# Forming the low parts of the first layer's weights on GpSimd, with a new written order for the start of the kernel

## Chip, cores and metric

One core of a Trainium2 chip runs the whole program. The metric is device time in microseconds. The kernel before was timed three times: 861.56, 856.57 and 857.43 us, median 857.43. A fourth execution, the profiled one, took 856.71 us; its span from the first to the last instruction is 854.8 us.

Engine names as the profile has them: PE is TensorE (matmul), PEld its weight loads, DVE is VectorE, ACT is ScalarE, POOL is GpSimd, SP is SyncE, which here issues the DMAs.

## What is computed

```
kv  = einsum('bhsd,bhse->bhde', k, v)            # b=4, h=8, s=576, d=64
o   = einsum('bhsd,bhde->bhse', q, kv)
x   = o / sqrt(mean(o*o, -1) + 1e-6) * g_norm    # -> 2304 tokens x 512
h   = x @ w_in1                                  # 512 x 2048
g   = h * tanh(softplus(h))                      # mish
x2  = g @ w_out1                                 # 2048 x 512
h2  = x2 @ w_in2;  g2 = max(h2,0) + alpha*min(h2,0)
out = g2 @ w_out2
```

The inputs come as 64-bit floats; the kernel reads them as pairs of 32-bit words.

## The kernel before

Every product of the two MLPs is made of three PE passes over fp32r operands, a rounded high part and the low part that is left: high x high, high x low, low x high (function `three`, lines 128 to 132). So each operand, weight or activation, needs a high part, which ACT forms by a rounding copy, and a low part, which is source minus high, one subtraction of a 128x512 tile.

A weight tile of 128x512 goes through these steps: a DMA brings its 64-bit words into a stage tile `ws`; ACT scales the high words (`w_scale`, L390, "A" in the written order); DVE puts the fp32 number together by three integer instructions (`w_bits`, L396, L397, L400, "D") in a tile `wf`, of which there are two in turn; ACT rounds it (`w_high`, L435, "H"); DVE subtracts (`w_low`, L439, "L"). Activations: mish is ACT's L505, which writes one of two tiles `n`; `g_split` rounds on ACT (L498) and subtracts on DVE (L499, the tile `gl`).

The tokens go in five blocks (512, 256, 512, 512, 512). In a block the first MLP runs over 16 slots, one for each 128 of the 2048 hidden units: slot s makes the first product of slot s (`mm1`, 12 matmuls), mish of slot s-1, the split of s-2 and the second product of s-4 (`mm2`, 12 matmuls). All weights of the first MLP are prepared in the first block, two tiles in each slot, (1, s+2) of the first layer in `mid` and (2, s-2) of the second in `last`, and kept in SBUF. `w_begin` and `w_end` (lines 443 to 454) hold a tile's high and low part back until the next tile has its bits. In slots 8 to 15 the attention of block 1 is made beside this (`hook`), with its own rows on DVE: L322 to L333 in slots 10 and 11, L345 and L363 in slots 13 and 14.

Ahead of slot 4 lies a start stage whose order is a written list, `START` (lines 44 to 49). Each entry is a letter for a step and its indices: K, k, T, t, O, s, M, l, n, f make the attention of block 0 for one pair of heads; x and y split the normed tokens (`x_split` rounds on ACT, L358; `x_low` subtracts on DVE, L363); A, D, H, L prepare a weight tile, where c0 to c3 are the first layer's weights for hidden units 0 to 511 (one tile for each 128 rows of w_in1, home `w1first`), w4 and w5 the next tiles of the first layer, u0 and u1 tiles of the second; Pcj is the three matmuls of token chunk c and slot j; g is mish and G its split. P3j needs x3 and the low parts of chunk 3.

Up to slot 20 (`MANUAL`) each engine's order is the written one. After that only PE's is, and a scheduler sets the others. GpSimd does little in the kernel before: some memory setting at the start, and subtractions in preparing the second MLP's weights from 227 us on.

Of the kernel before, what the change touches and what calls it, by code (L numbers as in the profile page):

```python
# [13 lines left out]
ALU = mybir.AluOpType  # L14
# [28 lines left out]
FIRST = "p0 c0 p1 c1 p2 p3 c2 c3 w4 u0 w5 u1".split()  # L43
START = """
W9 K0 k0 W1 T0 t0 W2 Ac0 O0 Dc0 s0 W2 K1 M0 k1 Hc0 Lc0 T1 l0 t1 n0 O1 V f0 K2 s1 x0 M1 k2 Ac1 y0 T2 l1
Dc1 t2 n1 O2 f1 K3 s2 Hc1 M2 k3 x1 Lc1 Ac2 T3 y1 l2 P01 Dc2 P02 t3 P12 n2 Hc2 O3 Ac3 f2 s3 M3 Lc2 x2
y2 P00 P03 Dc3 P10 P11 P13 l3 P20 P21 Z n3 Hc3 f3 P22 P23 Lc3 x3 Aw4 y3 Au0 Dw4 P30 P31 P32 P33 g0
G0 Hw4 Lw4 Du0 g1 G1 Hu0 Aw5 Lu0 g2 Dw5 Au1 Hw5 Du1 Lw5
""".split()


# [1 line left out]
def attn_moe_moe2(  # L53
# [30 lines left out]
    nc = tc.nc  # L84
# [41 lines left out]
    f32 = lambda t: t.bitcast(F32)  # L126

    def three(ps, lhs, rhs, start, stop, **kw):
        (lh, ll), (rh, rl) = lhs, rhs
        nc.tensor.matmul(ps, lh, rh, start=start, stop=False, **kw)  # L130
        nc.tensor.matmul(ps, lh, rl, start=False, stop=False, **kw)  # L131
        nc.tensor.matmul(ps, ll, rh, start=False, stop=stop, **kw)  # L132
# [3 lines left out]
    xh, xl = {}, {}  # L136
    at = {}
# [17 lines left out]
    def load_kv(b, p):  # L155
        R = S // KVJ
        for nm, src in (("k", k), ("v", v)):
            cols = 2 * KVJ * D
            t = room(nm, F32, cols) if b == 0 else kvp.tile([P, cols], F32, tag=nm, name=nm)
            t = t.rearrange("p (h j d) -> p h j d", h=2, j=KVJ)  # L160
            nc.sync.dma_start(
                out=t[:R], in_=src[b, 2 * p : 2 * p + 2, :, :].rearrange("h (p j) d -> p h j d", j=KVJ)
            )
            kvt[nm, b, p] = t[:R]
# [36 lines left out]
    def bank(tag, nm):  # L201
        if tag == "at":
            turn[0] += 1
            tag = f"at{turn[0] % 2}"
        pool = ps_h if tag == "h" else ps_a if tag[:2] == "at" else ps_acc
        return pool.tile([P, 512], F32, tag=tag, name=nm)
# [143 lines left out]
    def x_split(i, p, src):  # L350
        T = BLOCKS[i]
        if (i, 0) not in xh:
            x = xp.tile([P, 8 * TM], F32R, tag="x", name="x")
            for c in range(NP):
                xh[i, c] = x[:, 2 * c * TM : 2 * c * TM + T]
                xl[i, c] = x[:, (2 * c + 1) * TM : (2 * c + 1) * TM + T]
        h = xh[i, p]
        nc.scalar.copy(out=h, in_=src)  # L358
        if i:
            x_low(i, p, src)  # L360

    def x_low(i, p, src):
        nc.vector.tensor_tensor(out=xl[i, p], in0=src, in1=f32(xh[i, p]), op=ALU.subtract)  # L363

    def stage(nm, dt, cols):
        return st.tile([P, 2 * DM], dt, tag="ws", name=nm, bufs=3)[:, :cols]
# [58 lines left out]
    def w_parts(L, which, j):  # L425
        s = wst[L, which, j]
        if which:
            return *w_home(L, which, j), s
        w_home(L, 1, 0)
        w = w1[L, "first"]  # L430
        return w[:, :, 0, j, :], w[:, :, 1, j, :], s.rearrange("p (j f) -> p j f", j=EARLY)

    def w_high(L, which, j):
        h, _, s = w_parts(L, which, j)
        nc.scalar.copy(out=h, in_=s)  # L435

    def w_low(L, which, j):
        h, l, s = w_parts(L, which, j)
        nc.vector.tensor_tensor(out=l, in0=s, in1=f32(h), op=ALU.subtract)  # L439

    begun = []

    def w_end():
        while begun:
            w = begun.pop()
            w_high(*w)
            w_low(*w)

    def w_begin(*w):

# [12 lines left out]
    def at_slot(kk):  # L463
        i = kk // NJ
        return i, kk % NJ, BLOCKS[i]

    def mm1(kk, chunks=range(4)):
        i, j, T = at_slot(kk)
        if chunks[0] == 0:
            hps[kk] = bank({2: "at1", 3: "acc3"}.get(kk, "h"), "h")  # L470
        ps = hps[kk]
        wh, wl = w1[0, j]
        for c in chunks:
            cs = slice(c * P, (c + 1) * P)
            three(ps[:, :T], (wh[:, cs], wl[:, cs]), (xh[i, c], xl[i, c]), c == 0, c == NP - 1)
# [409 lines left out]
    for i in range(1, NB):  # L885
        h0, step, dk, do, dm, db = WHEN[i]
        h0 += (i - 1) * 2 * NJ
        for p in range(NP):
            h = h0 + p * step
# [71 lines left out]
    def slot(s):  # L961
        run(early, s)
        mm1(s)
        run(hook, 2 * s)
        run(after, s)
        run(late, s)
        front(s)
        run(mid, s)
        run(fin, s)
        back(s)  # L970
        run(hook, 2 * s + 1)
        run(last, s)
# [36 lines left out]
    def warm(n):  # L1009
# [18 lines left out]
        "f": f_ev,  # L1028
        "x": lambda p: x_split(0, p, at["x", p]),
        "y": lambda p: x_low(0, p, at["x", p]),  # L1030
        "A": w_scale,
        "D": w_bits,
        "H": w_high,
        "L": w_low,
        "P": lambda c, j: mm1(j, (c,)),
        "Z": lambda: nc.scalar.preload_act_table_set("mish"),
        "g": mish,
# [2 lines left out]
    with tc.manual_schedule():  # L1040
        nc.scalar.preload_act_table_set("abs_reciprocal_sqrt_and_small")
        for n in FIRST:
            if n[0] == "p":
                load_kv(0, int(n[1]))
                load_q(0, int(n[1]))
            else:
                load_w(0, code[n[0]], int(n[1:]), True)
            if n == "p1":
                for h in range(2):
                    nc.sync.dma_start(out=gcol[h * D : (h + 1) * D, :], in_=g_norm.rearrange("(p o) -> p o", o=1))  # L1050
        nc.sync.dma_start(out=acol, in_=alpha.rearrange("(j p) -> p j", p=P))
        make_identity(nc, ident)
        nc.vector.memset(ones_bd, 0.0)
        nc.vector.memset(ones_m, 0.0)
        for h in range(2):
            r = slice(h * D, (h + 1) * D)
            nc.vector.memset(ones_bd[r, r], 1.0 / D)
            nc.vector.memset(ones_m[r, 16 * h : 16 * h + 16], 1.0 / D)
        nc.vector.memset(epsb, EPS * 2.0**-SHIFT)
        nc.gpsimd.memset(keep[:, : 5 * P], 0.0)  # L1060
        nc.vector.memset(neglo, 0.0)
        for p in range(NP):
            for h in range(2):
                r = 32 * p + 16 * h
                rows = pick[p][:, h * D : (h + 1) * D]
                nc.vector.tensor_copy(out=rows, in_=ident[:, r : r + 1].to_broadcast([P, D]))
                nc.vector.tensor_tensor(
                    out=rows, in0=f32(rows), in1=ident[:, r + 1 : r + 2].to_broadcast([P, D]), op=ALU.add
                )
                nc.vector.tensor_tensor(out=neglo, in0=neglo, in1=ident[:, r + 1 : r + 2], op=ALU.subtract)  # L1070
        for n in START:
            if n[0] in "ADHL":
                w = (0, code[n[1]], int(n[2:]))
                first[n[0]](*w)
            else:
                first[n[0]](*(int(c) for c in n[1:]))
        begun.append((0, 2, 1))
        for s in range(EARLY, MANUAL):
            slot(s)
# [35 lines left out]
```

## Time and profile before

| | value |
|---|---|
| median of 3 runs | 857.43 us (856.57 to 861.56) |
| profiled execution | 856.71 us, span 854.8 us |
| PE busy | 832.7 us (97%) |
| DVE busy | 537.1 us (63%) |
| ACT busy | 314.1 us (37%) |
| POOL busy | 41.8 us (5%) |

The busy shares are means over the whole program. A change in the first block is read from the stretches of that block, and there from what PE waits for and who that one waits for. In the rows below, a timeline row shows the start in us, the duration in us, engine, line, operation, output <- inputs with shapes, and in brackets how long the engine had been idle and which engine's instruction released it. A row with x2 is two instructions merged. [...]

### The profile page before, as it was taken

The numbers are of one execution on the slowest core, as the hardware profiler recorded it, in microseconds if no ns is written. First come the engines' busy times: TensorE is split into PE (matmuls) and PEld (weight loads), VectorE is DVE, ScalarE is ACT, GpSimd is POOL, SyncE is SP. The second block draws the span as 40 slices with busy tenths as digits, with TensorE's granted clock in tenths as the row PEclk, the third lists the DMA queues.
The fourth block names the chain that finished last, engine by engine and source line by source line (L and its number), as shares of the span: only waits on it lengthen the run. The fifth ranks groups of instructions, "written<-read, shape, count | busy, mean of one in ns | idle before, by whom it ended". The sixth has DMA issues, their size and how long they took to land.

```text
span 854.8 us, 11671 instructions
## 1 busy us (share of the span) xinstructions
PE 832.7 (97%) x4408; PEld 711.5 (83%) x4408; DVE 537.1 (63%) x1017; ACT 314.1 (37%) x619; POOL 41.8 (5%) x52
## 2 busy tenths in 40 slices
PE   7999889989999999999999999999999999999997
PEld 5677668888878887888888888888988988998896
DVE  6988966372246242635697887889665568655644
ACT  4766445434333443234465323234211124111111
POOL 0000000000210303020300000000000000000000
PEclk9999999999999999999999999999999999999999
DMA  9766454414331233026996623241321231411212
GB/s 250 222 172 205 139 150 102 110 27 106 100 112 25 77 109 135 1 94 231 404 357 231 209 63 134 97 137 39 125 61 38 62 123 39 140 44 38 74 38 74
DMA packets 84744, 104.59 MB, mean 122 GB/s; under 512 B 34768, under 2 KB 58832, under 8 KB 84688
## 3 DMA queue, kind: packets, MB, share of 16 engines
q1 hardware_dynamic: 84688, 103.84, 39.2%
q8 instruction: 35, 0.57, 0.3%
q14 instruction: 21, 0.17, 0.1%
HBM read 79.70 MB, written 24.12 MB: 121 GB/s over the span
## 4 chain that ended last, share of the span: by engine, by line
PE 82%; DVE 8%; DMA 4%; SPq 2%; ACT 2%; issue 1%; DVEq 0%; ACTq 0%
PE acc L130 13%; PE acc L132 13%; PE acc L131 13%; PE h L130 7%; PE h L131 6%; PE h L132 6%; PE pp L130 6%; PE pp L132 6%; PE pp L131 6%; DMA v<-in_v_dram 2%; SPq L183 2%; PE kvps L214 1%; DVE wf L397 1%; DVE wf L400 1%; DMA k<-in_k_dram 1%
## 5 line engine op out<-in xcount | busy, mean ns | idle before, releaser
L130 PE MATMUL acc<-gh,w 128*128 128x512 f32 (+1 forms) x320 | 119.6, 374 | 0.8 <-ACT n L505 0.4
L132 PE MATMUL acc<-gh,w 128*128 128x512 f32 (+1 forms) x320 | 118.0, 369 | 0.0
L131 PE MATMUL acc<-gl,w 128*128 128x512 f32 (+1 forms) x320 | 117.9, 369 | 0.0
L499 DVE TENSOR_TENSOR gl<-n,gh 128x512 fp32r<-128x512 f32 (+1 forms) x80 | 52.2, 652 | 89.9 <-ACT gh L498 89.6
L130 PE MATMUL h<-x,w 128*128 128x512 f32 (+1 forms) x240 | 91.5, 381 | 5.6 <-ACT n L505 5.6
L132 PE MATMUL h<-x,w 128*128 128x512 f32 (+1 forms) x240 | 89.7, 374 | 0.6 <-DVE w L439 0.5
L131 PE MATMUL h<-x,w 128*128 128x512 f32 (+1 forms) x240 | 89.6, 373 | 0.0
L132 PE MATMUL acc<-w,g 128*128 128x512 f32 x216 | 85.4, 395 | 0.0
L498 ACT CAST gh<-n 128x512 fp32r<-128x512 f32 (+1 forms) x80 | 46.1, 577 | 100.4 <-PE acc L132 99.9
L766 ACT CAST g<-ty 128x384 fp32r<-128x384 f32 x48 | 24.7, 515 | 138.4 <-DVE ty L764 136.5
L130 PEld LDWEIGHTS acc<-gh,w 128*128 128x128 f32 x320 | 60.3, 188 | 11.9 <-ACT n L505 0.9
L132 PEld LDWEIGHTS acc<-gh,w 128*128 128x128 f32 x320 | 60.3, 188 | 10.6 <-DVE w L439 0.4
L131 PEld LDWEIGHTS acc<-gl,w 128*128 128x128 f32 x320 | 60.4, 189 | 9.6
L505 ACT ACTIVATE n<-h 128x512 f32<-128x512 f32 (+1 forms) x80 | 44.5, 556 | 45.3 <-DVE gl L499 44.6
L130 PEld LDWEIGHTS h<-x,w 128*128 128x128 f32 x240 | 45.9, 191 | 17.3 <-ACT n L505 6.9
L131 PE MATMUL acc<-w,g 128*128 128x512 f32 x144 | 56.6, 393 | 0.0
L131 PE MATMUL acc<-w,xb 128*128 128x512 f32 x144 | 56.6, 393 | 0.0
L130 PE MATMUL acc<-w,g 128*128 128x512 f32 x144 | 56.0, 389 | 0.0
L130 PE MATMUL acc<-w,xb 128*128 128x512 f32 x144 | 56.0, 389 | 0.0
L132 PEld LDWEIGHTS h<-x,w 128*128 128x128 f32 x240 | 45.9, 191 | 9.5 <-DVE w L439 1.6
L131 PEld LDWEIGHTS h<-x,w 128*128 128x128 f32 x240 | 45.8, 191 | 7.4
L132 PEld LDWEIGHTS acc<-w,g 128*128 128x128 f32 x216 | 40.5, 188 | 9.4 <-DVE g L767 0.9
(216 smaller groups left out, 1700.2 us busy)
## 6 DMA issues: line engine op xcount, KB each, us to landing
xb<-wd SPq DMA_DIRECT2D x72, 256.0 KB, 2.7
ws<-in_moe_w_out_dram SPq DMA_DIRECT2D x32, 512.0 KB, 4.3
ws<-in_moe_w_in_dram SPq DMA_DIRECT2D x16, 512.0 KB, 4.8
r<-in_moe_w_in_dram SPq DMA_DIRECT2D x12, 512.0 KB, 3.9
wd<-r SPq DMA_DIRECT2D x12, 512.0 KB, 2.6
w<-wd SPq DMA_DIRECT2D x12, 512.0 KB, 6.0
k<-in_k_dram SPq DMA_DIRECT2D x16, 288.0 KB, 3.8
v<-in_v_dram SPq DMA_DIRECT2D x16, 288.0 KB, 4.2
```

The source lines that it names most:

```text
L130: nc.tensor.matmul(ps, lh, rh, start=start, stop=False, **kw)
L131: nc.tensor.matmul(ps, lh, rl, start=False, stop=False, **kw)
L132: nc.tensor.matmul(ps, ll, rh, start=False, stop=stop, **kw)
L183: nc.sync.dma_start(out=t[r : r + 32, C * p0 : C * (p0 + n)].rearrange("p (b d) -> p b d", d=32), in_=q[b, h, s : s + C * n, d : d + 32].r ...
L214: nc.tensor.matmul(ps[hs, hs], kt[:, h, j, :], vt[:, h, j, :], start=(j == 0), stop=(j == KVJ - 1))
L397: nc.vector.scalar_tensor_tensor(out=si, in0=high, scalar=-0x80000000, in1=si, op0=ALU.bitwise_and, op1=ALU.bitwise_or)
L400: nc.vector.scalar_tensor_tensor(out=si, in0=high, scalar=3, in1=si, op0=ALU.logical_shift_left, op1=ALU.bitwise_or)
L498: nc.scalar.copy(out=gh, in_=g)
L499: nc.vector.tensor_tensor(out=gl, in0=g, in1=f32(gh), op=ALU.subtract)
L505: nc.scalar.activation(out=g, in_=hps.pop(kk)[:, :T], func=AF.Mish)
L766: nc.scalar.copy(out=h, in_=out)
```

## The change

Thirty-three subtractions go from DVE to GpSimd: the low parts of c1, c2, c3, w4, u0 and w5 in the start stage (new letter Q), two of the four token chunks' low parts (x1 and x2, new letter z), and every low part that `w_end` forms (u1 and the 24 tiles of slots 4 to 17). c0, x0 and x3 stay on DVE. `START` is written anew: P00 stands ahead of O2, the bits of w4 (Dw4) stand ahead of the norm of the last pair (n3, f3), and w4 and u0 get their high and low parts earlier as seen from the first mish.

```diff
 START = """
 W9 K0 k0 W1 T0 t0 W2 Ac0 O0 Dc0 s0 W2 K1 M0 k1 Hc0 Lc0 T1 l0 t1 n0 O1 V f0 K2 s1 x0 M1 k2 Ac1 y0 T2 l1
-Dc1 t2 n1 O2 f1 K3 s2 Hc1 M2 k3 x1 Lc1 Ac2 T3 y1 l2 P01 Dc2 P02 t3 P12 n2 Hc2 O3 Ac3 f2 s3 M3 Lc2 x2
-y2 P00 P03 Dc3 P10 P11 P13 l3 P20 P21 Z n3 Hc3 f3 P22 P23 Lc3 x3 Aw4 y3 Au0 Dw4 P30 P31 P32 P33 g0
-G0 Hw4 Lw4 Du0 g1 G1 Hu0 Aw5 Lu0 g2 Dw5 Au1 Hw5 Du1 Lw5
+t2 Dc1 P00 n1 O2 f1 K3 s2 Hc1 Qc1 M2 k3 x1 z1 Ac2 T3 P01 l2 t3 Dc2 P02 O3 Hc2 Qc2 n2 Ac3 f2 s3 P03 M3
+x2 z2 Aw4 Dc3 l3 P10 P11 P12 P13 Hc3 Qc3 Dw4 n3 f3 Z Au0 P20 P21 P22 P23 x3 y3 Hw4 Qw4 P30 P31 P32 P33
+Du0 Aw5 g0 G0 Hu0 Qu0 g1 Dw5 g2 G1 Au1 Hw5 Qw5 Du1
 """.split()
...
-    def x_low(i, p, src):
-        nc.vector.tensor_tensor(out=xl[i, p], in0=src, in1=f32(xh[i, p]), op=ALU.subtract)
+    def x_low(i, p, src, e=nc.vector):
+        e.tensor_tensor(out=xl[i, p], in0=src, in1=f32(xh[i, p]), op=ALU.subtract)
...
-    def w_low(L, which, j):
+    def w_low(L, which, j, e=nc.vector):
         h, l, s = w_parts(L, which, j)
-        nc.vector.tensor_tensor(out=l, in0=s, in1=f32(h), op=ALU.subtract)
+        e.tensor_tensor(out=l, in0=s, in1=f32(h), op=ALU.subtract)
...
             w_high(*w)
-            w_low(*w)
+            w_low(*w, nc.gpsimd)
...
+        "z": lambda p: x_low(0, p, at["x", p], nc.gpsimd),
...
+        "Q": lambda *w: w_low(*w, nc.gpsimd),
```

In DVE's order of the start stage, from the norm of head pair 2 (L305, L306) on, the difference is this (q is the normed tile, wf a weight being put together):

```order
 L305 SCALAR_TENSOR_TENSOR q<-u,q 128x512
 L306 SCALAR_TENSOR_TENSOR q<-ops,gneg,q 128x512
-L439 TENSOR_TENSOR w1first<-wf,w1first 128x4x128
-L363 TENSOR_TENSOR x<-q,x 128x512
+L396 TENSOR_SCALAR wf<-ws 128x512
+L397 SCALAR_TENSOR_TENSOR wf<-ws,wf 128x512
+L400 SCALAR_TENSOR_TENSOR wf<-ws,wf 128x512
```

The low parts of c2 and x2 are gone from this place. Two preparations, c3 and w4, now stand in a row ahead of the norm of pair 3, where one did.

In a slot of the first block DVE's rows stood like this before (two finished subtractions `w`, one weight's bits, the activation's low part `gl`, the next weight's bits):

```order
L439 TENSOR_TENSOR w_569<-wf,w_569 128x512
L439 TENSOR_TENSOR w_606<-wf,w_606 128x512
L396 TENSOR_SCALAR wf<-ws 128x512
L397 SCALAR_TENSOR_TENSOR wf<-ws,wf 128x512
L400 SCALAR_TENSOR_TENSOR wf<-ws,wf 128x512
L499 TENSOR_TENSOR gl<-n,gh 128x512
```

Both L439 rows are gone from DVE; L396, L397, L400, L499 and again L396 to L400 stand there without a break.

GpSimd's order, from its last memory setting on, begins with these rows (w_430 is w4, w_456 u0, w_472 w5):

```order
L1062 MEMSET keep 128x640
L439 TENSOR_TENSOR w1first<-wf,w1first 128x4x128
L363 TENSOR_TENSOR x<-q,x 128x512
L439 TENSOR_TENSOR w_430<-wf,w_430 128x512
L439 TENSOR_TENSOR w_456<-wf,w_456 128x512
L439 TENSOR_TENSOR w_472<-wf,w_472 128x512
```

The first two kinds of rows alternate as c1, x1, c2, x2, c3 in the program; 28 `w` rows follow and then the rows that were there before.

## Rows read from the trace of the kernel before

**Rows 1.** Stretches: start:end; busy us (rows) of PE, PEld, DVE, ACT, POOL; clock, DMA
```profile
28.40:37.70 9.30, 9.30 (x41) 7.33 (x39) 8.35 (x14) 7.17 (x12) 0.00 (x0) 1.00 0.56 149
37.70:46.70 9.00, 7.56 (x51) 5.15 (x50) 8.43 (x16) 6.44 (x12) 0.00 (x0) 1.00 0.32 117
46.70:84.00 37.30, 37.30 (x239) 29.96 (x236) 31.49 (x53) 24.31 (x53) 0.00 (x0) 1.00 0.73 207
84.00:97.00 13.00, 13.00 (x58) 10.72 (x58) 12.26 (x26) 4.86 (x9) 0.00 (x0) 1.00 0.43 135
97.00:119.70 22.70, 17.23 (x63) 12.71 (x62) 18.41 (x35) 11.61 (x23) 0.00 (x0) 0.86 0.49 148
```

**Rows 2.** Timeline of PE, the first matmul after its longest stop
```profile
116.69 0.64 PE L130 MATMUL h<-x,w 128*128 128x512 f32 x1 [2.76 <-ACT n L505]
```

**Rows 3.** Waits, PE from 20, others from 0 us: total us, times, longest
```profile
PE h L130 <- ACT n L505: 5.2, 4, 2.8
DVE w L439 <- ACT w L435: 5.8, 9, 0.9
SPq L378 <- DVE wf L400: 26.3, 10, 4.6
```

**Rows 4.** Instructions of tile w, first 140 us: durations in ns, min/median/max
```profile
L439 DVE TENSOR_TENSOR w<-wf,w x28: 681/688/694, 37.8 to 138.9; 128x512 fp32r<-128x512 f32 x28
```

**Rows 5.** Timeline of ACT and DVE in the start stage
```profile
22.95 0.70 ACT L390 ACTIVATE ws<-ws 128x512 f32<-128x512 f32 x1
...
32.78 0.75 DVE L306 SCALAR_TENSOR_TENSOR q<-ops,gneg,q 128x512 f32<-128x512 f32 x1
33.45 0.68 DVE L439 TENSOR_TENSOR w1first<-wf,w1first 128x512 fp32r<-128x512 f32 x1
33.57 0.62 ACT L358 CAST x<-q 128x512 fp32r<-128x512 f32 x1 [1.21 <-DVE q L306]
34.22 0.70 DVE L363 TENSOR_TENSOR x<-q,x 128x512 fp32r<-128x512 f32 x1
```

**Rows 6.** Timeline of DVE in slots 13 and 14
```profile
109.02 0.42 DVE L396 TENSOR_SCALAR wf<-ws 128x512 int32<-128x512 int32 x1
...
110.27 0.69 DVE L400 SCALAR_TENSOR_TENSOR wf<-ws,wf 128x512 int32<-128x512 int32 x1
110.88 0.68 DVE L499 TENSOR_TENSOR gl<-n,gh 128x512 fp32r<-128x512 f32 x1
111.48 0.47 DVE L345 SCALAR_TENSOR_TENSOR qT<-o,gcol,bps 128x256 f32<-128x256 f32 x1
...
117.18 0.69 DVE L439 TENSOR_TENSOR w<-wf,w 128x512 fp32r<-128x512 f32 x1 [0.58 <-ACT w L435]
```

**Rows 7.** Groups of POOL by form: busy us, mean ns of one | idle before
```profile
L576 POOL TENSOR_TENSOR r<-wf,r 128x512 fp32r<-128x512 f32 x10 | 13.2, 1319 | 55.8 <-ACT r L575 55.8
```

**Rows 8.** Timelines of POOL and DVE where both work, in later blocks
```profile
321.11 0.74 POOL L621 TENSOR_TENSOR r<-wf 128x256 f32<-128x256 f32 x1
321.22 1.17 DVE L249 TENSOR_TENSOR qs<-qT,qs 128x512 fp32r<-128x512 f32 x1 [0.83 <-ACT qs L248]
321.93 1.06 POOL L622 TENSOR_TENSOR wf<-r,wf 128x256 f32<-128x256 f32 x1
...
387.62 1.29 POOL L576 TENSOR_TENSOR r<-wf,r 128x512 fp32r<-128x512 f32 x1 [3.53 <-ACT r L575]
388.14 1.32 DVE L397 SCALAR_TENSOR_TENSOR xw<-xw 128x512 int32<-128x512 int32 x1 [1.40 <-ACT xw L390]
...
423.74 0.97 DVE L396 TENSOR_SCALAR xw<-xw 128x512 int32<-128x512 int32 x1
```

**Rows 9.** Timeline of PE: last chunk's first product, slot 4's first, slot 5's first
```profile
35.03 0.39 PE L130 MATMUL h<-x,w1first 128*128 128x512 f32 x1
...
37.75 0.48 PE L130 MATMUL h<-x,w 128*128 128x512 f32 x1
...
46.73 0.50 PE L130 MATMUL h<-x,w 128*128 128x512 f32 x1
```

## What I predict, before the run

> **What bounds the kernel now.** I read the table of stretches first, to find where TensorE (PE) stands still near the code that changes. From 46.7 to 84 us it is busy all the time, and VectorE (DVE) is busy 31.49 of 37.3 us. From 97 to 119.7 us PE is busy only 17.23 of 22.7 us, at a mean granted clock of 0.86, and from 37.7 to 46.7 us 7.56 of 9.0 us [rows 1]. So the first block has two places where time can be won, about 5.5 us and 1.4 us of standing still, and the lost clock. In the second place the matmuls that follow a stop last 0.64 us [rows 2] and stand at half speed, the 1.2 GHz level; a clock of 0.86 over 22.7 us means that about 28% of it was at half speed, so some 3.2 us of work were lost. Everything else in the program (the other 700 us) is not touched except by the order in which the scheduler then puts rows.
>
> The list of waits says who makes PE wait: the mish on ScalarE (ACT), 5.2 us in 4 pieces, the longest 2.8 us [rows 3]. The mish in turn waits for DVE, which frees its two `n` buffers with `gl` (L499). DVE works in written order, and `gl` stands in line behind the weight preparation. DVE itself waits for ACT to round a weight (L435) before it can form the low part (L439): 5.8 us in 9 pieces [rows 3]. So in these stretches DVE is what matters, and the reader should see its queue as the path.
>
> **The price that leaves DVE.** 33 subtractions go: 28 of `w` at 0.688 us [rows 4], three of `w1first` and two of `x` at the same price (0.68 and 0.70 us, [rows 5]). From start to start on a full DVE one takes 0.61 to 0.77 us [rows 5, 6]; I take 0.61 (0.67 in the start stage). By stretch: 8 before 46.7 us, 12 up to 84 us, 9 up to 119.7 us, 4 after.
>
> **The price that comes.** The same shape and types on GpSimd (POOL) take 1.32 us in ten cases [rows 7], 1.29 us undisturbed. POOL had nothing else to do there, so its own time costs nothing; each low part has at least one slot (over 6 us) until it is read. What costs is that the two engines exclude each other, and the trace shows it. A DVE subtraction that starts 0.11 us behind a POOL one takes 1.17 us instead of 0.69 and ends 0.54 us after POOL's end; POOL's next one, issued meanwhile, ends 0.60 us after DVE's end and takes 1.06 us for 0.74 us. L397 beside a 512-wide POOL row takes 1.32 us and ends 0.55 us after POOL's end. The shift L396 takes 0.97 us instead of 0.42 beside POOL [rows 6, 8]. So they alternate: POOL holds about 1.29 - (0.74 - 0.60) = 1.15 us, then DVE's op needs 0.55 us. On a full DVE the next row would have ended 0.79 us after the one before (0.10 gap and 0.69); with POOL between it ends 1.15 + 0.55 = 1.70 us after. **One POOL subtraction delays a full DVE by 0.9 us** and takes 0.61 us off it. The bounds are 0 (it falls into an idle time of DVE) and 0.9.
>
> Which DVE rows are held up is partly unknown: all rows seen beside POOL have two inputs in SBUF or are the fast shift. Rows with one input in PSUM (L301, L306, L345) never stand beside POOL in this trace; bounds 0 and 0.9 us. They differ from every blocked row in just that input, so I take 0 and keep 0.9 for the range. The Trainium skill (SBUF — State Buffer, "Who interferes with whom") says that a DVE instruction with at most one SBUF input outside the two-port modes does not contend with GpSimd. By that the sum stays as below; no run here shows it.
>
> **The start stage, up to 46.7 us.** DVE is full from 17 us on. Its last row on the way to the last chunk of tokens is L363 (`y3`), ending at 34.92 us [rows 5], and PE begins the last 12 of 48 products at 35.03 us, just behind it [rows 9]. Now five subtractions go ahead of it (-3.4), the bits of `w4` come in ahead of it (one preparation, L396 to L400, 1.86 us, [rows 6]), and two waits for ACT come into the open that they covered (the scaling of c2 on ACT, 0.4, the rounding of x3, 0.5, [rows 5]): 34.9 - 3.4 + 1.9 + 0.9 = 34.3 us undisturbed. Five POOL subtractions fall in here (c1, z1, c2, z2, c3). Walking through the written order, c1 holds up the shift of c2, z1 its L397, z2 the last row of c3 and c3 that of w4; c2 falls beside L306 and is free. Four times 0.9 gives 38.0 us. PE finishes 12 products (2.72 us from 35.03 to 37.75, [rows 9]) at about 40.6 us instead of 37.75: **2.9 us late**. But then w4 and u0 are ready, whose rounding and low part PE waits for today: from 37.75 to 46.73 us are 8.98 us [rows 9], of which 24 products at 0.227 us, a transposition (0.2) and a kv product (0.85) make 6.5 us. So 2.5 us of standing still go, and slot 5 begins at 40.6 + 6.5 = 47.1 instead of 46.73: **+0.4 us**. P00, moved ahead of O2, lies in a wait of PE for ACT and costs nothing; without that cover it would be 0.7 us.
>
> **46.7 to 84 us.** DVE needed 31.5 us; less 12 x 0.61 = 24.2. Of the 37.3 us that is 65%, so POOL meets a busy DVE about two times in three: 12 x 0.9 x 0.65 = 7.0, sum 31.2, at worst 35.0. Both are under 37.3 us, PE stays the bound: **0**. New waits, for the second `wf` buffer that POOL now frees, come a whole preparation later and lie under it.
>
> **84 to 119.7 us.** DVE is full, but for waits. Nine subtractions (5.5) go and about 1.3 us of waits for L435, as the 0.58 ahead of L439 at 117.18 [rows 6]: -6.8. Nine POOL rows come at 0.9; of the 28.9 us left, L345 (four times 0.47, [rows 6]) and waits make about 5 us in which POOL is free, so 83% hit: +6.8. What remains is that `gl` stands directly behind one preparation and no longer behind two subtractions and a wait (1.7 us), of which POOL takes back 0.9: once, where DVE falls behind, PE is served **0.8 us** earlier. SyncE's loads follow, as the weight loads wait for L400 on DVE (26.3 us in 10 pieces, [rows 3]), so nothing is lost behind it. The four subtractions after 119.7 us and the scheduler's changed order of a few casts and q loads lie where DVE has idle time: 0, bounds -1 and +1.
>
> Sum: the profiled execution has 856.71 us (span 854.8); +0.4 + 0 + 0 - 0.8 = 856.3. The median of three runs is 857.43, 0.7 above it: **857.0 us**, no change that can be measured.
>
> **Rivals.** *Faster, POOL falls into gaps.* If the nine rows of the third stretch meet only waits and PSUM rows, 6.8 us of DVE's path go there; PE can use all of it, having 5.5 us of waits and 3.2 us of slow clock. In the start stage two hits instead of four win 1.8 us on the walk: -1.4 in place of +0.4. Sum 857.4 - 6.8 - 1.4 = 849.2. For it: DVE waits for ACT often, and those waits are where POOL starts. Against: POOL starts 0.6 us after a preparation ends, when DVE goes straight to the next row.
> *Slower, exclusion.* One mechanism: every POOL row meets a busy DVE, PSUM rows too. Start stage: five hits, +1.3. 46.7 to 84 us: 12 x 0.9 = 10.8, demand 35.0 plus some 3 us carried over from the start is 38 for 37.3: +0.7. Third stretch: 8.1 - 6.8 + 0.9 x 4 (L345) = +4.9. Further, the stop of PE before the last chunk (35.0 to 37.3 us or more) is as long as the 2.76 us stop after which the clock is at half [rows 2]; 12 products at half speed for a time like there cost 1.6 us more. Sum 857.4 + 8.5 = 865.9. It decides from the point where a POOL row costs more than the 0.75 us (0.61 and its share of the wait) that it saves. For it: [rows 8]; against: DVE's idle times.
> *Half of that.* The clock falls in the start stage but the rest stands as forecast: 858.6, inside the forecast's range.
>
> **Chances.** Forecast with its own range 853 to 861: 0.62. Faster rival: 0.16. Slower rival: 0.19. Something else: 0.03. The range for 8 in 10 reaches towards both rivals, 850 to 865. A measurement of this kernel tells about 1% from no change (8.6 us). Beyond 848.9 lies the smaller part of the faster rival, 0.09; beyond 866.0 half of the slower one and a little more, 0.13; within, 0.78.
>
> **What would show it.** Right: POOL has 33 rows of 1.3 to 1.9 us between 22 and 140 us; DVE's mean L397 and L400 there go from 0.69 to 0.9 or more; `y3` ends near 38 us, slot 5 begins near 47 us; PE idles in 97 to 119.7 us about as much as before. Wrong: L396 to L400 keep 0.42 and 0.69 us while POOL works (no exclusion, the faster rival and more), or PE idles in 46.7 to 84 us (the slower one), or the clock there is under 1.00.

## The result, and the profile of the changed kernel

The changed kernel took **869.75 us** (median; 867.62 to 871.44), the kernel before 857.38 us in the same comparison. The ratio is 1.0135, 95% interval 1.0101 to 1.0169, so 8.7 to 14.5 us more. It is slower, outside the forecast's range (850 to 865) and above even the time of the slower rival (865.9). The profiled execution took 870.11 us, its span is 868.1 us (before 854.8).

The page's line of busy time per engine, changed kernel (us, share of the span, instructions):

```profile
PE 838.8 (97%) x4408; PEld 715.8 (82%) x4408; DVE 544.1 (63%) x984; ACT 314.4 (36%) x619; POOL 86.9 (10%) x85
```

DVE has 33 instructions fewer (984 for 1017). They would have taken 33 x 0.688 = 22.7 us [rows 4], yet DVE is busy 7.0 us more. So the rows that stayed grew by 29.7 us, which is **0.90 us for each of the 33 POOL rows**. That is an upper figure, because the busy time counts once where neighbouring rows overlap (the L439 at 33.45 us begins before L306 ends at 33.53, [rows 5]): the durations of DVE's rows, added up, grew by 27.9 us, 0.85 us for each POOL row. Groups of instructions by form, 20 to 147 us (busy us, mean ns of one | idle before it); POOL's group is of 0 to 160 us. First the kernel before, then the changed one:

```profile
L400 DVE SCALAR_TENSOR_TENSOR wf<-ws,wf 128x512 int32<-128x512 int32 x31 | 21.5, 692 | 1.1
L397 DVE SCALAR_TENSOR_TENSOR wf<-ws,wf 128x512 int32<-128x512 int32 x30 | 20.8, 692 | 3.3 <-ACT ws L390 0.7
L396 DVE TENSOR_SCALAR wf<-ws 128x512 int32<-128x512 int32 x30 | 12.6, 421 | 1.3 <-DMA ws<-in_moe_w_in_dram 1.2
```

```profile
L397 DVE SCALAR_TENSOR_TENSOR wf<-ws,wf 128x512 int32<-128x512 int32 x30 | 30.5, 1017 | 5.0 <-ACT ws L390 2.0 <-ACT q L294 0.5
L400 DVE SCALAR_TENSOR_TENSOR wf<-ws,wf 128x512 int32<-128x512 int32 x30 | 26.5, 885 | 1.0
L396 DVE TENSOR_SCALAR wf<-ws 128x512 int32<-128x512 int32 x30 | 18.6, 621 | 5.7 <-DMA ws<-in_moe_w_in_dram 5.7
...
L439 POOL TENSOR_TENSOR w<-wf,w 128x512 fp32r<-128x512 f32 x28 | 38.0, 1358 | 78.2 <-ACT w L435 74.2 <-DMA ws<-in_moe_w_in_dram 4.0
```

The three rows that put a weight together carry most of it, 21.5 us: L397 went from 692 to 1017 ns, L400 from 692 to 885, L396 from 421 to 621. Most of the rest is on L499, L305, L328 and L329, where they stood beside a POOL row. POOL's own rows are near the price taken for them, 1358 ns for 1319 [rows 7].

How a row is hit is seen in one slot. Timelines of DVE and POOL, changed kernel:

```profile
67.32 0.42 DVE L396 TENSOR_SCALAR wf<-ws 128x512 int32<-128x512 int32 x1
67.84 1.60 DVE L397 SCALAR_TENSOR_TENSOR wf<-ws,wf 128x512 int32<-128x512 int32 x1
69.47 0.69 DVE L400 SCALAR_TENSOR_TENSOR wf<-ws,wf 128x512 int32<-128x512 int32 x1
71.17 1.29 DVE L396 TENSOR_SCALAR wf<-ws 128x512 int32<-128x512 int32 x1 [1.01 <-DMA ws<-in_moe_w_in_dram]
...
67.53 1.36 POOL L439 TENSOR_TENSOR w<-wf,w 128x512 fp32r<-128x512 f32 x1 [2.54 <-ACT w L435]
70.90 1.29 POOL L439 TENSOR_TENSOR w<-wf,w 128x512 fp32r<-128x512 f32 x1 [2.00 <-DMA ws<-in_moe_w_in_dram]
```

POOL starts at 67.53, released by ACT's rounding; DVE's L397, issued next, takes 1.60 us instead of 0.69 and ends 0.55 us after POOL's end. POOL's second row starts at 70.90 in a gap in which DVE waits for a weight load; but it is still at work when the load lands, and the shift L396 takes 1.29 us instead of 0.42. So a row that starts in a gap of DVE delays it too, unless more of the gap is left than POOL's own 1.3 us. Of the 33 rows, 20 began while DVE worked. Of the 13 that began in a gap, 12 had 0.02 to 0.70 us of it left and lengthened DVE's next row. One, at 133.14 us, had 1.64 us left and met no row of DVE. Timelines of DVE and POOL:

```profile
131.71 0.69 DVE L400 SCALAR_TENSOR_TENSOR wf<-ws,wf 128x512 int32<-128x512 int32 x1
134.77 0.69 DVE L499 TENSOR_TENSOR gl<-n,gh 128x512 fp32r<-128x512 f32 x1 [2.37 <-ACT gh L498]
...
133.14 1.28 POOL L439 TENSOR_TENSOR w<-wf,w 128x512 fp32r<-128x512 f32 x1 [4.42 <-ACT w L435]
```

The stretches of [rows 1] in the changed kernel:

```profile
28.40:37.70 9.30, 6.72 (x26) 4.73 (x26) 8.84 (x11) 5.22 (x8) 3.64 (x3) 1.00 0.53 122
37.70:46.70 9.00, 7.87 (x22) 6.00 (x23) 8.16 (x11) 6.25 (x11) 2.85 (x3) 0.62 0.42 146
46.70:84.00 37.30, 36.71 (x249) 29.69 (x248) 31.15 (x37) 23.02 (x49) 14.94 (x11) 1.00 0.62 174
84.00:97.00 13.00, 13.00 (x65) 10.27 (x64) 11.31 (x16) 7.55 (x14) 5.09 (x4) 1.00 0.48 150
97.00:119.70 22.70, 16.12 (x61) 11.73 (x60) 19.27 (x30) 9.05 (x17) 7.17 (x6) 0.92 0.43 137
```

From 46.7 to 84 us DVE does 37 rows in the time in which it did 53, and its busy time is the same (31.15 for 31.49). Waits, changed kernel, 20 to 150 us (total us, times, longest):

```profile
ACT w L435 <- DVE wf L400: 24.7, 19, 3.5
...
PE h L130 <- ACT n L505: 8.5, 4, 3.4
DVE gl L499 <- ACT gh L498: 5.9, 4, 2.4
DVE wf L396 <- DMA ws<-in_moe_w_in_dram: 5.7, 5, 1.4
...
PE acc L132 <- POOL w L439: 1.3, 2, 0.6
```

DVE's 5.8 us of waits for the rounding [rows 3] are gone, as meant. In their place it waits for weight loads (5.7 us, 1.2 before) and for ACT's rounding of the activations (5.9 us, 1.2 before), and PE waits longer for mish (8.5 us for 5.2 [rows 3]). PE's waits for the low parts themselves are small (1.3 us).

The start, timeline of DVE (answering [rows 5]) and of POOL:

```profile
23.31 1.18 DVE L396 TENSOR_SCALAR wf<-ws 128x512 int32<-128x512 int32 x1
25.01 1.19 DVE L397 SCALAR_TENSOR_TENSOR wf<-ws,wf 128x512 int32<-128x512 int32 x1 [0.51 <-ACT q L294]
...
27.68 1.80 DVE L305 SCALAR_TENSOR_TENSOR q<-u,q 128x512 f32<-128x512 f32 x1
...
31.43 1.67 DVE L400 SCALAR_TENSOR_TENSOR wf<-ws,wf 128x512 int32<-128x512 int32 x1
...
34.27 1.67 DVE L400 SCALAR_TENSOR_TENSOR wf<-ws,wf 128x512 int32<-128x512 int32 x1
...
38.81 0.69 DVE L363 TENSOR_TENSOR x<-q,x 128x512 fp32r<-128x512 f32 x1 [0.68 <-ACT x L358]
...
27.66 1.27 POOL L439 TENSOR_TENSOR w1first<-wf,w1first 128x512 fp32r<-128x512 f32 x1 [2.01 <-ACT w1first L435]
```

`y3` (38.81) ends at 39.50; all five low parts held a row of DVE (the five rows above it). Timeline of PE, the places of [rows 9] and, last, that of [rows 2]:

```profile
38.83 0.80 PE L130 MATMUL h<-x,w1first 128*128 128x512 f32 x1 [3.43 <-ACT x L358]
...
40.57 0.63 PE L130 MATMUL h<-x,w1first 128*128 128x512 f32 x1
...
44.41 0.53 PE L130 MATMUL h<-x,w 128*128 128x512 f32 x1
...
107.96 0.50 PE L130 MATMUL h<-x,w 128*128 128x512 f32 x1 [3.44 <-ACT n L505]
```

PE stands still for 3.43 us ahead of the last chunk, and the 12 products behind it last 5.58 us (38.83 to 44.41) instead of 2.72 [rows 9]: matmuls of 0.63 us, half speed, in a stretch whose clock is 0.62. Slot 5 begins at 51.20 us.

Executions differ by when their first data land. I therefore count from DVE's L301 of the third head pair (20.19 us before, 20.71 after). By that count the changed kernel is later by 4.1 us at `y3`, 4.0 at slot 5, 4.6 at the mish of slot 8 (77.48 and 82.60), 6.9 at that of slot 10 (88.39 and 95.85), 10.3 at that of slot 14 (119.78 and 130.57), and 11.5 at the L339 near 180 us (179.26 and 191.26). So some 4 us come in the start, some 6 between 75 and 130 us, and 1.2 from there to 180 us. By the same count the span ends 12.8 us later, so 1.3 us come behind 180 us, where the granted clock is 0.72 from 190 to 196 us and 1.00 at the same place before (178 to 184 us).

### The profile page after: what moved, and what is told of

It reads as the page before. It is cut to its first block, busy times and chain, and to the rows that moved or that the text cites. A ratio compares the mean times of both kernels' runs of the same rounds, so it can differ in the third digit from the quotient of the medians.

```text
span 868.1 us, 11721 instructions
## 1 busy us (share of the span) xinstructions
PE 838.8 (97%) x4408; PEld 715.8 (82%) x4408; DVE 544.1 (63%) x984; ACT 314.4 (36%) x619; POOL 86.9 (10%) x85
## 4 chain that ended last, share of the span: by engine, by line
PE 77%; DVE 11%; DMA 6%; ACT 2%; SPq 2%; issue 2%; DVEq 0%; ACTq 0%
PE acc L131 13%; PE acc L132 13%; PE acc L130 13%; PE h L130 6%; PE h L131 6%; PE h L132 6%; PE pp L130 6%; PE pp L132 6%; PE pp L131 6%; DMA v<-in_v_dram 2%; DMA ws<-in_moe_w_in_dram 2%; DVE wf L397 2%; DVE wf L400 2%; SPq L193 1%; DVE wf L396 1%
## 5 line engine op out<-in xcount | busy, mean ns | idle before, releaser
L130 PE MATMUL acc<-gh,w 128*128 128x512 f32 (+1 forms) x320 | 119.7, 374 | 0.9 <-ACT w L435 0.9
L132 PE MATMUL acc<-gh,w 128*128 128x512 f32 (+1 forms) x320 | 118.2, 369 | 1.3 <-POOL w L439 1.3
L499 DVE TENSOR_TENSOR gl<-n,gh 128x512 fp32r<-128x512 f32 (+1 forms) x80 | 55.0, 688 | 96.4 <-ACT gh L498 96.2
L132 PE MATMUL h<-x,w 128*128 128x512 f32 (+1 forms) x240 | 90.1, 375 | 0.5 <-POOL w L439 0.5
L132 PE MATMUL acc<-w,g 128*128 128x512 f32 x216 | 85.4, 395 | 0.0
L498 ACT CAST gh<-n 128x512 fp32r<-128x512 f32 (+1 forms) x80 | 46.2, 577 | 107.1 <-PE acc L132 106.7
L132 PEld LDWEIGHTS acc<-gh,w 128*128 128x128 f32 x320 | 60.3, 188 | 12.6 <-POOL w L439 2.5
L130 PEld LDWEIGHTS h<-x,w 128*128 128x128 f32 x240 | 46.4, 193 | 20.7 <-ACT n L505 10.6
L132 PEld LDWEIGHTS h<-x,w 128*128 128x128 f32 x240 | 46.5, 194 | 8.9 <-POOL w L439 0.9
L131 PEld LDWEIGHTS h<-x,w 128*128 128x128 f32 x240 | 46.8, 195 | 7.6
L132 PEld LDWEIGHTS acc<-w,g 128*128 128x128 f32 x216 | 40.5, 188 | 9.4 <-DVE g L767 0.9
```

Source lines behind the costliest of these rows:

```text
L498: nc.scalar.copy(out=gh, in_=g)
L499: nc.vector.tensor_tensor(out=gl, in0=g, in1=f32(gh), op=ALU.subtract)
```

## Experiments

**The new written order, everything on DVE** (e1_order_only; from the changed kernel):

```diff
-            w_low(*w, nc.gpsimd)
+            w_low(*w)
...
-        "z": lambda p: x_low(0, p, at["x", p], nc.gpsimd),
+        "z": lambda p: x_low(0, p, at["x", p]),
...
-        "Q": lambda *w: w_low(*w, nc.gpsimd),
+        "Q": w_low,
```

> The changed kernel with every subtraction back on VectorE: the new written order of the start stage alone. Theory (VectorE and GpSimd exclude each other, which makes the last token chunk late, and the stop of TensorE halves its clock): without GpSimd the last chunk's low part comes near 37 us instead of 39.5, the stop ahead of its products is about 2 us, slot 5 begins between 46 and 48 us, total 857 to 860 us. Rival (the new order itself costs the start's 4.5 us): slot 5 near 51 us, total 862 us.

Measured: 859.53 us, ratio 1.0025 (1.0016 to 1.0035). Timelines of DVE and PE:

```profile
39.89 0.69 DVE L363 TENSOR_TENSOR x<-q,x 128x512 fp32r<-128x512 f32 x1 [0.68 <-ACT x L358]
...
39.91 0.49 PE L130 MATMUL h<-x,w1first 128*128 128x512 f32 x1 [4.02 <-ACT x L358]
```

`y3` stands 18.6 us behind L301, 4.6 later than before: with the low parts on DVE, the order that puts the bits of w4 and the low parts ahead of `y3` costs that alone, since each subtraction now waits openly for its rounding (four waits of 0.68 or 0.69 us). Slot 5 is 3.7 us late, but the end only 2.1: 3.5 us came back at 125 us, where the scheduler placed a transposition (L246) that waits for its q load behind a split instead of ahead of it.

**GpSimd in the slots only, written order of before** (e2_slots_only; from the kernel before):

```diff
-            w_low(*w)
+            w_low(*w, nc.gpsimd)
```

> The kernel before with its old start stage, all of it on VectorE; only the 25 low parts of the slots go to GpSimd. Theory (exclusion): nearly each of the 25 rows holds up a VectorE row by 0.9 us, no loss up to about 80 us, then 6 to 9 us, total 863 to 866 us. Rival (GpSimd's low parts simply come 0.6 us later and TensorE waits for them): 2 to 3 us, total 860 us, VectorE rows not lengthened.

Measured: 865.92 us, ratio 1.0095 (1.0079 to 1.0111). The page's line:

```profile
PE 836.6 (97%) x4408; PEld 714.4 (83%) x4408; DVE 541.7 (63%) x992; ACT 314.2 (36%) x619; POOL 75.6 (9%) x77
```

25 rows left DVE, whose other rows grew by 541.7 - 537.1 + 17.2 = 21.8 us, 0.87 each (0.80 by the durations added up). One of the 25, at 129.77 us, met no row of DVE. Counted from L301, slot 5 is where it was, the mish of slot 8 is 1.2 us late, of slot 10 3.9, of slot 14 7.2. So two thirds of the changed kernel's loss come from `w_end` alone.

**The start only** (e3_start_only; the changed kernel with `w_low(*w)` in `w_end`):

> The changed kernel with the 25 low parts of the slots back on VectorE: new start stage with its eight GpSimd rows alone. Theory: slot 5 near 51 us with the half clock in the last chunk's products, then as the kernel before: total 861 to 862.5 us. If the slots' loss came from starting late and not from GpSimd, total 866 us or more.

Measured: 861.20 us, ratio 1.0053 (1.0032 to 1.0074), that is +3.7 us. `y3` is 4.0 us late, slot 5 3.2 us. With e2's +8.4 the sum is +12.1, for +12.4 measured: the two halves add. That they add so closely is partly luck, because the scheduler placed L246 (see e1) behind the split in e2 and in the changed kernel, but ahead of it, as before, in e3.

**The old order with its start's low parts on GpSimd** (e4_old_order_pool; from the kernel before, only the entries shown and their counterparts for c2, c3, w4, u0, w5):

```diff
-... x1 Lc1 Ac2 T3 y1 ...
+... x1 Qc1 Ac2 T3 z1 ...
```

> The kernel before with its old written order, the same eight subtractions of the start stage on GpSimd, the slots on VectorE. Theory (exclusion): five held rows at 0.9 us against five at 0.6 to 0.7 taken off, the last chunk's low part 1 to 1.5 us later than 34.9 us, no long stop and full clock, total 858 to 860 us. Rival (order is the cost, exclusion is free): 857 us or less.

Measured: 857.39 us, ratio 0.9998 (0.9986 to 1.001). `y3` is 1.2 us late, slot 5 1.7 us and the mish of slot 14 still 1.7 us; at that of slot 15 it is 0.2 us early, since here too the scheduler placed L246 behind the split. So the exclusion costs 1.7 us in the old order as well, and the equal time is, by this trace, the scheduler's doing. With e1 (3.7 us at slot 5 by the order alone) both order and exclusion cost in the start.

**A GpSimd subtraction whose result nobody uses** (e5_shadow_sub; from the kernel before; all real work stays on DVE):

```diff
             w_low(*w)
+            h, _, s = w_parts(*w)
+            nc.gpsimd.tensor_tensor(out=s, in0=s, in1=f32(h), op=ALU.subtract)
```

> The kernel before with all its work on VectorE, and beside it a GpSimd subtraction of the same shape after each of the 25 low parts of the slots, whose result nobody reads (it overwrites the finished source tile). It costs the exclusion alone, with no low part later than before. Theory (exclusion): VectorE rows next to a GpSimd row take about 0.9 us longer, nothing is taken off VectorE, so 9 rows between 84 and 120 us cost 8 us and the twelve before some more: total 866 to 873 us. Rival (late low parts, no exclusion): 857 to 859 us.

**The same with a fill instead** (e6_shadow_set), which writes the same tile and reads nothing:

```diff
+            nc.gpsimd.memset(s, 0.0)
```

> The same kernel, but the 25 GpSimd rows beside it only write (a fill of the finished source tile, 128x512) and read nothing. If the exclusion is one of reading, VectorE's rows with two inputs keep 0.69 us and only the fast shift (0.42 us) may be held: total 857 to 860 us. If GpSimd holds VectorE whatever it does, each row costs its own duration of about 0.5 us: total 860 to 864 us.

Measured: the subtraction 876.03 us, ratio 1.0212 (1.0193 to 1.0231), DVE's busy time 553.8 us; the fill 857.29 us, ratio 0.9986 (0.9971 to 1.0001), DVE's busy time 537.6 us (537.1 before). Timelines of DVE and POOL with the subtraction, and POOL's group with the fill:

```profile
81.10 1.50 DVE L396 TENSOR_SCALAR wf<-ws 128x512 int32<-128x512 int32 x1 [1.19 <-POOL wf L449]
...
79.28 3.04 POOL L449 TENSOR_TENSOR wf<-wf,w 128x512 f32<-128x512 f32 x2 [5.01 <-DVE w L439]
```

```profile
L449 POOL MEMSET wf<- 128x512 f32 x25 | 14.1, 564 | 128.9 <-DVE w L439 128.9
```

What costs is that POOL reads while DVE works. Part of e5's loss is another thing, the wait for the `wf` tile (1.19 us in the row, 7.1 us in all). The Trainium skill (SBUF — State Buffer, "Who interferes with whom") says that a DVE instruction with two SBUF inputs contends with a GpSimd instruction that reads SBUF and not with one that only writes it; these two runs agree, at 16.7 us more DVE time for 25 reading rows and 0.5 for 25 writing ones. The fill isn't free for every row: two of the shifts L396 beside one took 0.59 and 0.79 us for 0.42.

e5 also has a row with one input in PSUM that ran wholly beside a POOL row. Timelines of DVE and POOL:

```profile
136.15 0.47 DVE L345 SCALAR_TENSOR_TENSOR qT<-o,gcol,bps 128x256 f32<-128x256 f32 x1
...
135.77 1.62 POOL L449 TENSOR_TENSOR wf<-wf,w 128x512 f32<-128x512 f32 x1 [1.29 <-DVE w L439]
```

It kept its 0.47 us while POOL's row went on to 137.39 us. That is one row, and it bears out the 0 that the forecast took for L345.

**Keeping PE busy ahead of the last chunk** (e7_warm; the changed kernel with matmuls ahead of `x3` whose sums nobody uses):

```diff
-... P20 P21 P22 P23 x3 y3 ...
+... P20 P21 P22 P23 w x3 y3 ...
...
+        "w": lambda: warm(20, "acc0"),
```

> The changed kernel with 20 spare small matmuls on TensorE in the stop ahead of the last token chunk's products (about 3 of the 3.4 us). Theory (the stop costs the clock): the 12 products take 2.7 us instead of 5.6, slot 4 begins 2.5 to 2.9 us earlier, near 41.7 us; the total gains less, because VectorE sets the pace afterwards: 867 to 869 us. Rival (the slow products have another cause): they still take 5 us or more, total 869.5 us or more.

Measured: 869.27 us, ratio 1.0136 to before (1.0113 to 1.0159), as the changed kernel. The stretch, and slot 5's first product on PE:

```profile
37.70:46.70 9.00, 9.00 (x51) 7.72 (x50) 8.07 (x12) 6.76 (x13) 3.06 (x3) 1.00 0.32 113
```

```profile
48.88 0.50 PE L130 MATMUL h<-x,w 128*128 128x512 f32 x1
```

The clock stays at 1.00, the 12 products take 2.84 us and slot 5 begins 2.1 us earlier, counted from L301; 0.8 us of it is left at the mish of slot 9 (88.04 for 89.05 us) and nothing at 149 us. The half speed is real, but DVE sets the pace behind it.

**Half the dose** (e12_second_only; e2 with only the second layer's low parts on GpSimd, which turned out to be 15 rows, not the 12 of the expectation):

```diff
+            w_low(*w, nc.gpsimd if w[1] == 2 else nc.vector)
```

> Half the dose of e2_slots_only: the written order of before, and in the slots only the second layer's low parts (12 of the 25 that w_end forms) on GpSimd, the first layer's 13 stay on VectorE. Theory 'each row held': every one of the 12 lengthens a VectorE row by about 0.9 us, so VectorE's busy time is by 12 x (0.90 - 0.69) = 2.5 us above before, and the time is about half of e2's +8.4 us: 861 to 862.5. Rival 'threshold': VectorE's work in a slot passes the 6.5 us of TensorE only when both rows of a slot are held, then half the dose costs under 1.5 us: 857 to 859. Rival 'the first layer's row is the costly one' (it starts beside the next slot's split): no more than 1 us, as the threshold, but VectorE's rows beside GpSimd keep 0.7 us.

Measured: 860.79 us, ratio 1.0035 (1.0021 to 1.0049), +3.0 us by the ratio. The page's line:

```profile
PE 834.6 (97%) x4408; PEld 713.0 (83%) x4408; DVE 536.9 (63%) x1002; ACT 314.4 (37%) x619; POOL 61.5 (7%) x67
```

DVE's other rows grew by 536.9 - 537.1 + 10.3 = 10.1 us, 0.67 per POOL row: two rows now fall wholly into waits of DVE, with 1.44 and 1.68 us of the wait left, and others in part. The cost is 0.20 us per row against 0.34 in e2. It lies between the two theories: no clean threshold, but more than in proportion.

**w4's bits behind `y3`** (e11_w4_later; from the changed kernel):

```diff
-... Hc3 Qc3 Dw4 n3 f3 Z Au0 P20 P21 P22 P23 x3 y3 Hw4 ...
+... Hc3 Qc3 n3 f3 Z Au0 P20 P21 P22 P23 x3 y3 Dw4 Hw4 ...
```

> The changed kernel with one entry of the written order moved: the bits of w4 (Dw4) stand behind y3 and no longer ahead of the norm of the last head pair. Theory: this entry is what makes y3 late, together with the GpSimd row of c3 that it meets, so y3 ends 1.9 to 2.8 us earlier than in the changed kernel and the last 12 products of the start with it; but VectorE has the same rows to do until slot 5, so at mish 8 to 10 at most 1 us of it is left, and the time is 868.5 to 870. Rival 'the start is the path': what y3 wins stays to the end, 866.5 to 868. Rival 'w4 then comes too late': slot 4 starts no earlier than in the changed kernel, 870 or more.

Measured: 868.37 us, ratio 1.0136 to before (1.0107 to 1.0165). Timeline of PE, slot 5's first product:

```profile
47.82 0.50 PE L130 MATMUL h<-x,w 128*128 128x512 f32 x1
```

`y3` comes 2.6 us earlier and slot 5 3.2 us earlier, counted from L301, so this entry made `y3` late. In the profiled execution some 2 us of it last to 130 us and its span is 3.2 us shorter; in the timed runs the ratio does not differ from the changed kernel's. How much of the start's loss lasts to the end stays open: 3.7 us by e3, none by e7, and this run doesn't decide.

**Fills in place of all GpSimd subtractions**, in the slots (e13_slots_fill, from e2) and in the changed kernel (e14_after_fill); these low parts are left out:

```diff
+        if e is nc.gpsimd:
+            nc.gpsimd.memset(f32(l), 0.0)
+            return
         e.tensor_tensor(out=l, in0=s, in1=f32(h), op=ALU.subtract)
```

> e2_slots_only with every GpSimd subtraction of the slots replaced by a GpSimd fill of the same low part with zeros (so the low parts are left out of the sums; GpSimd reads nothing, VectorE does no subtraction either). Theory 'reading is the whole cost': VectorE's rows keep 0.42 and 0.69 us, its busy time falls by 25 x 0.69 = 17 us to about 520, and the time falls from e2's 866 to 857 or under: 849 to 856, since PE's waits for mish (5.2 us) and part of its slow clock go. Rival 'another engine's low part and the changed order cost by themselves': 858 to 864 although VectorE's rows are short. Rival 'VectorE does not set the pace, weight loads do': 856 to 858.

> The changed kernel with all 33 GpSimd subtractions replaced by fills with zeros in the same places (these low parts are left out; GpSimd reads nothing). Theory 'reading is the whole cost of the slots, the written order that of the start': y3 ends 2.5 to 4 us earlier than in the changed kernel (39.5 us there), slot 5 begins near 47 to 48 us, VectorE's busy time is about 514 us, and the time is within 2 us of e13_slots_fill, 850 to 858. Rival 'the start's order costs even without the exclusion': 3 us or more above e13_slots_fill. Rival 'other than reading': 860 or more.

Measured: 855.12 us, ratio 0.9959 (0.9942 to 0.9977), and 853.97 us, ratio 0.9958 (0.9945 to 0.9971). The page's line of each, e13 first, then e13's last stretch of [rows 1], and DVE's `y3` in e14 (its L366 is L363 of the kernel before, as lines were added):

```profile
PE 831.5 (97%) x4408; PEld 712.2 (83%) x4408; DVE 522.9 (61%) x992; ACT 313.9 (37%) x619; POOL 55.6 (7%) x77
...
97.00:119.70 22.70, 18.88 (x82) 14.78 (x82) 16.46 (x31) 12.38 (x25) 0.00 (x0) 1.00 0.52 157
```

```profile
PE 833.2 (98%) x4408; PEld 713.7 (84%) x4408; DVE 522.3 (61%) x984; ACT 312.8 (37%) x619; POOL 58.2 (7%) x85
...
39.18 0.69 DVE L366 TENSOR_TENSOR x<-q,x 128x512 fp32r<-128x512 f32 x1 [0.69 <-ACT x L358]
```

Both kernels are faster than before, by 3.5 us, and DVE's weight rows keep their 0.42 and 0.69 us, but for one shift in each kernel (0.75 and 0.69 us). In the profiled execution of e14 the L301 of the third pair stands at 25.12 us, so `y3` is 14.1 us behind it, as in the kernel before (14.0), and slot 5 24.1 us, 2.5 us less than before. So the new order by itself is no loss once the five subtractions cost DVE nothing.

That L301 comes 4.9 us later than before is the fills' own doing, not that of late data. From 1.82 us on they run in a row, and a cast of DVE in the setup is held. Timelines of DVE, before and e14:

```profile
1.42 0.51 DVE L1066 CAST picks<-keep 128x64 fp32r<-128x64 f32 x1
...
1.42 4.70 DVE L1074 CAST picks<-keep 128x64 fp32r<-128x64 f32 x1
```

DVE's first two copies behind it (L224) come at 9.84 us instead of 6.23. So e14's time holds some 4 us that the changed kernel doesn't pay. From 853.97 to 869.75 are 15.8 us, and the 33 reading rows cost at least that; counted from L301 to the end of the span it is 19.1 us (847.4 and 828.3, with 834.6 before). 10.8 us are the slots' 25 (855.12 to 865.92). One caution: the fills wait for no rounding, and nearly all were done before 50 us. So they take the lateness of the low parts away as well, and in the slots POOL had nothing to do beside DVE's rows. PE's waits for POOL in the changed kernel bound the lateness, 1.3 us ahead of L132 in the second product and 0.5 in the first.

**Two attempts at a faster kernel.** A late q tile's first transposition (L246) kept behind the split (e9_late_transpose):

```diff
-            add(hook, h, t_ev, i, p)
+            if i == 2 and p == 1:
+                add(hook, h, behind, t_ev, i, p)
+            else:
+                add(hook, h, t_ev, i, p)
```

> The kernel before, with one transposition of block 2's second q tile (L246) tied behind the rows written ahead of it, so that the scheduler can't put it ahead of a gl row on VectorE, where it waits 3.0 us for its DMA. Theory (this place, which the new programs changed by the scheduler's doing, gives back part of their loss): the mish after it comes 3 us earlier, total 854 to 855.5 us. Rival (the wait goes over to the next step of that attention): 857 us.

The low part of the slot's first-layer weight written behind the split of the activations (e8_gl_first), and both together (e10_both):

```diff
-            add(mid, j + 3, w_end)
+            add(low, j + 3, w_end)
...
         back(s)
+        run(low, s)
```

> The kernel before, all subtractions on VectorE, with one thing moved: the low part of the slot's first-layer weight is written behind the split of the activations (gl) and no longer ahead of it. So VectorE does gl while ScalarE still rounds that weight. Theory: part of VectorE's 5.8 us of waits for that rounding goes, and PE's waits for mish (5.2 us) with it: 853 to 856, and mish 14 is 2 to 4 us earlier than before's 119.8 us. Rival 'the waits only move' (VectorE then waits for the next weight load, which comes as late as L400 lets it): 856.5 to 858.

> e8_gl_first and e9_late_transpose together: the split ahead of the first layer's low part, and the first transposition of a late q tile kept behind the split of slot 13. Theory: both act on the same stretch (100 to 130 us), so together no more than the better one and a little: 853 to 856. Rival: what they win there is given back by 180 us, as in e9: 856 to 858.

Measured: e9 856.52 us, ratio 0.9993 (0.9974 to 1.0013); e8 859.00, 1.0025 (1.0005 to 1.0045); e10 858.73, 1.001 (0.9992 to 1.0027). e8 is read by its times alone. In e9 the mish behind the moved row is 3.1 us earlier, counted from L301, and 1.7 us are left at the L339 near 180 us; the time shows no gain that can be measured. In e10 the longest stop of PE between 97 and 120 us is 2.25 us, for 2.76 [rows 2], and PE gets a new stop of 1.39 us at 156 us. No version that computes everything beats the kernel before.

## Why the prediction was wrong, step by step

**The price of one row was right.** 0.9 us of delay was forecast, and 0.90 (changed kernel) and 0.87 (e2) were measured by busy time, 0.85 and 0.80 by the durations. POOL's own 1.3 us were right, too, and that PE hardly waits for the low parts.

**The share of rows that are hit was wrong; this step failed.** "so POOL meets a busy DVE about two times in three" took DVE's mean busy share, and 83% in the third stretch, and counted the other rows as free. As a statement on where rows begin it came out: 20 of 33 began while DVE worked. But 32 of 33 lengthened a DVE row. A row takes 1.3 us, and where it began in a wait of DVE at most 0.70 us of the wait was left in all cases but one, so it was still reading when DVE's next row came (70.90 us). The forecast compared shares of time where the length of the row had to be compared with what was left of the wait. For that reason the faster rival, POOL in the gaps, is refuted.

**What the removal gains was oversized; this step failed too, and it weighs more.** For the third stretch the forecast took 6.8 us off, nine subtractions and the waits for L435, as if all of it were PE's wait. The fills show the removal by itself. From DVE's split (L499) of slot 4 to that of slot 14 DVE has the same rows but for 18 subtractions. That stretch, columns as in [rows 1], in the kernel before, the changed kernel and e13:

```profile
61.98:130.47 68.49, 62.84 (x319) 49.52 (x318) 55.64 (x102) 35.56 (x71) 0.00 (x0) 0.95 0.56 159
66.71:140.48 73.77, 63.18 (x318) 49.56 (x316) 57.64 (x84) 35.42 (x70) 23.47 (x18) 0.95 0.53 150
63.26:127.81 64.55, 59.30 (x318) 47.68 (x317) 44.73 (x84) 35.44 (x71) 0.00 (x0) 1.00 0.59 169
```

In e13 DVE's busy time falls by 10.9 us and the stretch by only 3.9. The waits for L435 (4.3 us) go, but waits for weight loads (0.2 to 5.5 us), for ACT's rounding of the activations (0 to 3.2) and for its scaled words (0.2 to 2.4) come, and DVE's idle time grows from 12.9 to 19.8 us. In the changed kernel the lengthened rows come on top (13.2 us), and the stretch is 9.2 us longer than with the fills. From the mish of slot 8 to that of slot 14, nearly the third stretch, e13 gains 3.2 us where the forecast had 6.8, and e2, which differs from it only in what GpSimd does, is 9.2 us behind it where the forecast had 6.8.

**46.7 to 84 us was sized 0** and is +0.7 by the count from L301 at slot 8, +1.2 in e2. With every row hit the demand is 24.2 + 10.8 = 35.0 us of 37.3, the forecast's own worst case. It left out that late weight preparations free the stage tiles late, so that the next loads come late: DVE's waits for them went from 1.2 to 5.7 us. In the changed kernel PE's only stop of note there, 0.59 us at 81.19 us, is for a load of v. That this is the chain is read from the waits, no run takes it alone.

**84 to 119.7 us was sized -0.8** and is some +5.7 (4.6 at slot 8, 10.3 at slot 14), +6.0 in e2. The slower rival had +4.9 for this stretch, but 3.6 of it by way of L345 being held, and L345 kept its time (474 and 470 ns): here it never stood beside a POOL row, and in e5, where one did, it wasn't held. What carried it instead is that the waits for L435 that DVE lost came back as waits for weight loads, for scaled words and for ACT's L498, as worked out above, and PE's stops ahead of the first product grew (3.44, 1.43 and 3.13 us).

**What the offload would have been worth** was oversized in the faster rival too: it gave -8.2 us, and the fills give -3.5. For e14, where the fills cost some 4 us in the setup, it is 6.3 us by the count from L301. DVE's path is only in part PE's wait.

**The start was sized +0.4** and is +4.0 at slot 5. The undisturbed walk (34.3 us for the end of `y3`, 0.6 earlier than before) was near: e14 has `y3` as in the kernel before. The hits were five and not four: c2 fell beside L305 (1.80 us) and not beside L306 as the walk had it, which is most of the 1.0 us by which `y3` missed its 3.1. The larger term is the half speed of the 12 products, 2.9 us, which the forecast had at nothing and the slower rival at 1.6. (Its sum is also a little short: 34.3 and four times 0.9 are 37.9, and 12 products behind that end at 40.7, not 40.6.) Stalls behind it went as forecast: from slot 4's first product to slot 5's are 6.8 us, for 6.5 worked out. That the 2.9 us matter little in the end (e7) was no part of the forecast.

**The order that the scheduler sets anew** was bounded by 1 us either way. Locally it is worth 3.5 us (e1, e9: L246 ahead of or behind a split at 125 us); most of that is given back before the end.

**P00 ahead of O2** isn't seen to cost anything, though no run takes it alone. **The PSUM rows**: none of L301, L306 and L345 ran beside a POOL row in the changed kernel. L345 did in e5 and kept its 0.47 us, and DVE's two copies from PSUM (L224, 22.83 to 23.28 us beside POOL's row from 22.93 us on) kept their 0.45 us together. L301 and L306 stay open.

**Where the right answer stood.** The slower rival, with a chance of 0.19, had the mechanism, every row hit, and a sum of +8.5; measured were +12.4. Its terms were +2.9, +0.7 and +4.9 for the three stretches, and 4.0, 0.7 and 5.7 were read from the trace; the other 2 us or so come behind 130 us, where it had nothing. That its third term is near is luck, since 3.6 of the 4.9 stood for rows that weren't held.

## What to carry to other kernels

Where a helper engine and the crowded one exclude each other, compare the length of the helper's row with what is left of the wait in which it starts. Here 1.3 us had to fit into 0.02 to 0.70 us, and a mean idle share said nothing about that. Before moving it, let the helper do the same operation with a result nobody reads, and then a write-only one: together they tell what sharing costs. Put write-only operations in place of the moved ones, and they tell what the move could bring at the most. Don't take the freed engine's time off the total: look for what it waits for next (here loads, roundings and scaled words).

## What the runs showed of the hardware

A GpSimd fill of 128x512 beside DVE's rows cost DVE 0.02 us each (e6, 25 fills, 0.564 us each); a subtraction of the same tile that reads two tiles cost 0.67 (e5), 0.87 (e2) and 0.90 us (changed kernel) by DVE's busy time. Fills in a row held one cast of DVE for 4.70 us instead of 0.51 (e14). A DVE row with one input in PSUM kept its 0.47 us beside a GpSimd subtraction (e5, L345, one row). In the 9 us from 37.70 us on, 1.1 us before the end of a stop of PE of 3.43 us, the granted clock was 0.62, that is mostly the 1.2 GHz level; it was 1.00 where filler matmuls had taken the place of the stop (e7).
